# Attention and spectral mixing in one kernel: weights of groups 0 to 2 in four rows a partition, mode products in eight tiles, spectra through a selecting table

## The chip, the cores and the metric

The kernel runs on one core of a Trainium2 chip. The metric is the device time of one execution in microseconds, the median over runs; one more execution was taken with the hardware profiler, and the profile and trace are of that one. Weights, queries, keys and values lie in HBM as float32 and are cast to 16 bits by the transfers.

## The reference

An attention over 8 batches, 8 heads, 576 tokens of width 64, with a bias from a running sum of `s`, feeds a mixing in frequency and a dense layer:

```python
scores = scale * q @ k.T + minimum(-(cum[i] - cum[j]), 0)   # causal; cum = cumsum(maximum(s, 0))
x = softmax(scores) @ v                                     # heads side by side: (8, 576, 512)
X = rfft(x, axis=1)[:, :64]                                 # 64 modes
Y[m] = X[m] @ (w_r[m] + 1j * w_i[m])                        # per mode, 512 x 512, real and imaginary
u = x + irfft(Y, n=576, axis=1)
out = u + maximum(u @ w_ch, 0)
```

`w_r` and `w_i` are 64 x 512 x 512 each, 134 MB together, and are read once.

## The kernel before, in words

**Steps.** The 512 columns are cut into four groups `g` of 128 (two heads each). A main loop runs over 32 steps `n`, eight batches `b` for each group. A step computes the scores of two heads (`scores`, L439 to L459), their product with the values (`av`, L491 to L497, which leaves `x_all`), the transposes of queries and keys for the next step (`transposes`, L400, copied out at L404) and, one step late, the spectrum of what it produced (`fft`, L512 and L522). The order within the step is written out by hand in program order; every engine takes its instructions in that order. Queries and keys come for two steps at a time, into two buffers `qk`.

**Spectrum.** `fft` multiplies the batch's `x_all` (576 tokens by 128 columns) by a table `Ff_sb` of sines, cosines and negative sines, even modes and odd modes in two halves, even columns and odd columns of `x` in two tiles of 64 output rows. Four copies place the result in `xs`: one half of the partitions holds even modes, the other odd modes, and the other half of each column range is zero. So one matrix product over 128 partitions serves two modes, each with two rows of the weights a partition.

**Mode products.** `modes(g, c)` multiplies the spectra of group `g` by the weights of eight modes (chunk `c` of eight): 16 matmuls of 128 rows by 32 columns, streaming 512 columns of weights, on the four column tiles of TensorE (L532). The result, one PSUM bank, is copied or added into `y_acc` (L550, L552). Two banks `aux` are shared by spectra and mode products. The products of group `g` are dealt over the steps of group `g + 1` (`mode_steps`): four chunks in its first step, the others one a step; those of the last group follow the loop, with the inverse transform, the dense layer and the outputs.

**Weights.** A tile `w_sb` holds eight modes of one of `w_r` and `w_i` for one group, 1 MB, in two transfers of 512 KB (`loads_w`): one to partitions 0 to 63, one to 64 to 127, two rows a partition, 64 partitions of four blocks of 2,048 written bytes. The first four tiles go to places that are used later for something else (`x_all`, `y_acc`), the others to three rings of five, three and one tiles. All casting transfers are issued by GpSimd (POOL) at L272, in program order, interleaved by a plan (`on_chip`) with the loads of queries, keys (`qk`) and values (`vr`, `v`). The framework gives POOL's transfers eight completion counters in turn, so an issue waits until the transfer eight before it has landed; it also waits until the buffer that it writes is free. SP issues the constants, one row of running sums a step (L387) and the outputs.

The lines of the profile are those of the listing that follows.

Of the kernel before, what the change touches and what calls it, by code (L numbers as in the profile page):

```python
# [10 lines left out]
FP32 = mybir.dt.float32  # L11
FP16 = mybir.dt.float16
# [7 lines left out]
def kernel(  # L20
# [38 lines left out]
    NK = RV + RV // 2  # L59
    HM = NM // 2  # L60
# [20 lines left out]
    Ff_np = np.zeros((SP, 3 * NM), dtype=np.float16)  # L81
    for h in range(2):
        for i, f in enumerate((np.sin(ang), np.cos(ang), -np.sin(ang))):
            Ff_np[:S, (3 * h + i) * HM : (3 * h + i + 1) * HM] = f[:, h::2]
# [3 lines left out]
    G_np[:, 1, :S] = -(cmv[:, None] * np.sin(ang.T))  # L88
    G_np = np.ascontiguousarray(G_np.reshape(P, SP)[:, :S].astype(np.float16))
# [5 lines left out]
    Ff_np = np.ascontiguousarray(Ff_np.reshape(NT, P, 3 * NM).transpose(1, 0, 2).reshape(P, -1))  # L95
# [15 lines left out]

    xs = [gp.tile([P, 2, 2, 2, 2, B, HM], BF16, name=f"xs{i}") for i in range(2)]
    xs_flat = [t.rearrange("p q k h r b m -> p (q k h r b m)") for t in xs]
    ident16h = gp.tile([P, P], FP16, name="ident16h")
    Ff_sb = gp.tile([P, NT, 3 * NM], FP16, name="Ff_sb")
# [41 lines left out]
    ident16 = ap_.tile([P, P], BF16, name="ident16")  # L157
    negm = ap_.tile([P, NMB + NMA + NL + 59], BF16, name="negm")
# [61 lines left out]
    wq = [(g, c, ri) for g in range(NG) for c in range(NCK) for ri in range(2)]  # L220
# [7 lines left out]
    whole = [xg[:, : 2 * HU], ya[:, HU : 3 * HU], xg[:, 2 * HU : 4 * HU]]  # L228
    whole = [e.rearrange("p (m e) -> p m e", e=DM) for e in whole]
# [12 lines left out]
    def loads_w(upto):  # L242
        todo = []
        while 2 * len(wt) < min(upto, 2 * len(wq)):
            k = len(wt)
            g, c, ri = key = wq[k]
            i = ring_of(k)
            if i is None:
                halves_, t = early[k], whole[k] if k < len(whole) else None
            else:  # L250
                t = (wpool, wpool2, wpool3)[i].tile([P, UM, DM], BF16, name="w_sb", tag="w")
                halves_ = [t[:, x * WM : x * WM + WM] for x in range(2)]
            if k == len(wq) - 1:
                t = None
            src = (moe_w_r, moe_w_i)[ri]
            for m0, m1, d in [(0, MC, t)] if t is not None else [(0, WM, halves_[0]), (WM, MC, halves_[1])]:
                for h in range(2):
                    first = 1 if ri == 1 and c == 0 and m0 + h == 0 else 0
                    todo.append((
                        d[HP * h : HP * h + HP, 2 * first :].rearrange("p (m q) e -> p m (q e)", q=2),  # L260
                        src[
                            c * MC + m0 + h + 2 * first : c * MC + m1 : 2, g * P : (g + 1) * P, :
                        ].rearrange("m (p q) e -> p m (q e)", q=2),
                    ))
            wt[key] = halves_
        return todo
# [88 lines left out]
    nc.vector.tensor_copy(out=ident16, in_=ident16h)  # L355
    for i in range(NQ):
        nc.vector.memset(kt[i][D : D + 1], 1.0)
# [145 lines left out]

    def fft(n):
        if n < 0:
            return
        g, b = divmod(n, B)
        ps = auxpool.tile([P, 2, 3 * HM], FP32, name="ft_ps", tag="aux")
        for T in range(NT):
            nT = tails[T]  # L510
            for q_ in range(2):
                nc.tensor.matmul(  # L512
                    ps[HP * q_ : HP * q_ + HP].rearrange("p h f -> p (h f)"),
                    x_all[:nT, g, b, T, q_::2], Ff_sb[:nT, T, :],
                    start=(T == 0), stop=(T == NT - 1),
                    tile_position=(0, HP * q_), skip_group_check=True,
                )
        for h in range(2):
            for q_ in range(2):
                a = ps[HP * q_ : HP * q_ + HP, h, : 2 * HM].rearrange("p (r m) -> p r m", r=2)  # L520
                a = bass.AP(tensor=a.tensor, offset=a.offset, ap=[a.ap[0], [HM, 2]] + list(a.ap[1:]))
                nc.vector.tensor_copy(out=xs[g % 2][HP * h : HP * h + HP, q_, :, h, :, b, :], in_=a)  # L522

    def modes(g, c, meanwhile=None):


        ps = auxpool.tile([P, DM], FP32, name="yp", tag="aux")
        cols = xs[g % 2].rearrange("p q k h r b m -> p q k (h r b) m")

        def product(ri, q_, cg):  # L530
            k0 = HP if ri == 1 and c == 0 and cg == 0 else 0
            nc.tensor.matmul(  # L532
                ps[32 * cg : 32 * cg + 32, :],
                cols[k0:, q_, 1 - ri, :, c * MC // 2 + cg],
                wt[(g, c, ri)][cg // 2][k0:, 2 * (cg % 2) + q_, :],
                start=(ri == 0 and q_ == 0), stop=(ri == 1 and q_ == 1),
                tile_position=(k0, 32 * cg), skip_group_check=True,
            )

        for x in range(4):  # L540
            ri, y = divmod(x, 2)
            if meanwhile and x in meanwhile:
                meanwhile[x]()
            for z in range(4):
                if meanwhile:
                    product(ri, z // 2, 2 * y + z % 2)
                else:
                    product(ri, y, z)
        if g == 0:
            nc.vector.tensor_copy(out=y_acc[:, c, :], in_=ps)  # L550
        elif g < NG - 1:
            nc.vector.tensor_tensor(out=y_acc[:, c, :], in0=ps, in1=y_acc[:, c, :], op=ALU.add)  # L552
        else:
            yb = spool.tile([P, DM], FP16, name="y_sb", tag="y")
            for cols in halves if c == NCK - 1 else [slice(0, DM)]:
                nc.vector.tensor_tensor(
                    out=yb[:, cols], in0=ps[:, cols], in1=y_acc[:, c, cols], op=ALU.add
                )
            if c >= NCK - 1:
                spread(c, 0, yb)  # L560
            return yb
# [62 lines left out]
    def mode_products(n, half=None):  # L624
        cs = mode_steps.get(n, [])
        for c in cs if half is None else cs[2 * half : 2 * half + 2]:
            modes(c // NCK, c % NCK)

    with tc.tile_pool(name="sc_psum", bufs=2, space=PSUM) as scpool, \
# [8 lines left out]
        for n in range(N):  # L638
            if n in (0, 2):
                nc.vector.memset(xs_flat[n // 2].bitcast(FP32), 0.0)  # L640
# [7 lines left out]
            if n and n % B == 0:  # L648
# [3 lines left out]
                av(n, 0)  # L652
                mode_products(n, 0)
                transposes(n + 1, 0)
                mode_products(n, 1)
                transposes(n + 1, 1)
# [10 lines left out]
            av(n, 0)  # L667
            if i is not None:
# [5 lines left out]
        fft(N - 1)  # L674
    load(loads_w(2 * len(wq)))
# [26 lines left out]
    places += [None, None, old[:, 4 * DM : 8 * DM]]  # L702
# [236 lines left out]
    def first_u():  # L939
# [5 lines left out]
        out=mark[:1], in_=wt[(NG - 1, NCK - 1, 1)][1][HP : HP + 1, WM - 1, :2]  # L945
# [101 lines left out]
```

## Time and profile before

| | |
|---|---|
| runs | 437.28, 437.50, 437.96 us, median 437.5 |
| the profiled execution | 437.52 us, of which the span of its instructions is 435.8 |
| TensorE busy (PE) | 375.4 us, 86% of the span |
| VectorE busy (DVE) | 260.1 us, 60% |
| ScalarE busy (ACT) | 247.1 us, 57% |
| GpSimd busy (POOL) | 141.7 us, 33% |
| transfers of POOL's queue (q0) | 52,560 packets, 81.28 MB written |
| HBM | 163.37 MB read, 9.51 MB written |
| w_r transfers of 512 KB to `w_sb` | 60, 16.5 us from issue to landing in the median |

Rows that give a stretch of time name its start and end, its length, the busy time of PE, PE's weight loads, DVE, ACT and POOL with the number of instructions, the clock granted to TensorE, the share of the 16 DMA engines that packets took, and the GB/s written. Packets overlap on an engine, so that share can pass 1. GB/s count written bytes; casting transfers read twice as many. A row of instructions gives start, length, engine, line, what is written and read, the shapes, how many, and in brackets the idle time before and what ended it. A row of a DMA queue gives packets, MB and their share of 16 engines.

### The profile page before, as it was taken

What the parts mean: (1) busy time and instruction counts of PE and PEld (TensorE: products, weight loads), DVE (VectorE), ACT (ScalarE), POOL (GpSimd) and SP (SyncE); (2) the same over time, 40 slices, a digit from 0 to 9 for tenths busy, and PEclk for the clock granted to TensorE, in tenths of its full rate; (3) what the DMA queues carried; (4) which work ended last, traced back from release to release, by engine and by line L of the source; (5) the groups of instructions that cost most, each with busy time, mean ns of one, the idle gap of its engine ahead of it and who ended that gap; (6) DMA issues with size and microseconds to landing.
All of it is one profiled execution on the core that took longest, in us unless ns stands there. A gap on an engine that the chain in (4) does not pass through costs nothing. (4 is left out here: it accounts for less than half of the span.)

```text
span 435.8 us, 11322 instructions
## 1 busy us (share of the span) xinstructions
PE 375.4 (86%) x4731; PEld 215.4 (49%) x4731; DVE 260.1 (60%) x605; ACT 247.1 (57%) x552; POOL 141.7 (33%) x216
## 2 busy tenths in 40 slices
PE   1699999989999978996496979999998798887994
PEld 1366666556666645654263635555555456442441
DVE  7757767566667665673264446566665654471795
ACT  1387777727767736665163725565565145430895
POOL 6454243141333222322323222322322322210483
PEclk9999999999999998998598878999999999999999
DMA  8999999999999999999999999999999999996698
GB/s 160 208 208 207 208 209 208 212 211 209 209 208 210 207 211 211 210 210 209 208 209 209 210 212 210 209 211 210 212 212 211 212 210 211 212 215 126 209 381 327
DMA packets 59548, 93.14 MB, mean 214 GB/s; under 512 B 8222, under 2 KB 18202, under 8 KB 59498
## 3 DMA queue, kind: packets, MB, share of 16 engines
q0 software_dynamic: 52560, 81.28, 102.9%
q1 hardware_dynamic: 6938, 11.15, 7.3%
q8 instruction: 37, 0.61, 0.5%
q14 instruction: 13, 0.11, 0.1%
HBM read 163.37 MB, written 9.51 MB: 397 GB/s over the span
## 5 line engine op out<-in xcount | busy, mean ns | idle before, releaser
L459 ACT ACTIVATE p_sb<-sc_ps,cumt_sb 128x320 f16<-128x320 f32 (+1 forms) x384 | 161.2, 518 | 31.3 <-PE sc_ps L450 31.3
L450 PE MATMUL sc_ps<-qt,kt 128*64 128x256 bf16 (+3 forms) x640 | 98.4, 301 | 8.8 <-ACT kt L404 8.7
L450 PEld LDWEIGHTS <-kt 128*128 128x128 bf16 (+1 forms) x640 | 50.9, 126 | 72.3 <-issue 38.7
L272 POOL DMA_DIRECT2D w_sb<-in_moe_w_i_dram x62 | 38.3, 619 | 91.3 <-PE yp L532 34.5
L404 DVE COPY qt<-tr_ps 64x576 bf16<-64x576 bf16 x64 | 47.7, 745 | 28.1 <-PE tr_ps L400 28.1
L272 POOL DMA_DIRECT2D w_sb<-in_moe_w_r_dram x60 | 37.0, 619 | 84.4 <-DMA w_sb<-in_moe_w_r_dram 27.2
L496 DVE RECIPROCAL rcp<-av_ps 128x5 f32<-128x5 f32 x64 | 12.5, 195 | 75.5 <-PE av_ps L491 74.5
L439 PE MATMUL sc_ps<-negm,ident 128*128 128x512 bf16 x128 | 52.1, 407 | 0.0
L400 PE MATMUL tr_ps<-ident,qk 64*64 64x64 bf16 x1152 | 32.5, 200 | 18.0 <-DMA qk<-in_k_dram 7.4
L491 PEld LDWEIGHTS <-p_sb 128*128 128x128 f16 x1088 | 42.2, 100 | 8.6 <-issue 3.8
L404 ACT COPY kt<-tr_ps 64x576 bf16<-64x576 bf16 x32 | 22.8, 713 | 37.6 <-DVE qt L404 36.9
L532 PE MATMUL yp<-w_sb,xs 128*32 128x512 bf16 (+1 forms) x480 | 37.9, 406 | 5.3 <-DMA w_sb<-in_moe_w_i_dram 3.6
L421 ACT ACTIVATE p<-sc_ps,cumt 128x64 f16<-128x64 f32 x32 | 10.0, 313 | 54.8 <-PE sc_ps L417 54.8
L400 PEld LDWEIGHTS <-qk 64*64 64x64 bf16 x1152 | 25.0, 114 | 31.7 <-issue 9.0
L522 DVE CAST xs<-ft_ps 64x128 bf16<-64x128 f32 x128 | 36.7, 287 | 6.1 <-PE ft_ps L512 4.7
L442 PE MATMUL sc_ps<-negm,ident 128*128 128x256 bf16 x128 | 36.6, 286 | 0.0
L491 PE MATMUL av_ps<-va,p_sb 128*128 128x65 f16 x768 | 35.9, 196 | 0.0
L497 DVE TENSOR_TENSOR x_all<-av_ps,rcp 128x320 f16<-128x320 f32 x64 | 31.5, 492 | 2.2
L491 PE MATMUL av_ps<-vb,p_sb 128*128 128x65 f16 x320 | 26.6, 198 | 3.8 <-DVE vb L375 3.8
L532 PEld LDWEIGHTS <-xs 128*32 128x32 bf16 (+1 forms) x512 | 17.8, 145 | 19.7 <-DMA w_sb<-in_moe_w_i_dram 6.4
L512 PE MATMUL ft_ps<-Ff_sb,x_all 128*64 128x192 f16 (+1 forms) x320 | 24.0, 263 | 0.8 <-DVE x_all L497 0.8
L404 DVE COPY kt<-tr_ps 64x576 bf16<-64x576 bf16 x32 | 24.4, 763 | 0.4
(120 smaller groups left out, 478.0 us busy)
## 6 DMA issues: line engine op xcount, KB each, us to landing
w_sb<-in_moe_w_r_dram POOLq DMA_DIRECT2D x60, 512.0 KB, 16.5
w_sb<-in_moe_w_i_dram POOLq DMA_DIRECT2D x55, 512.0 KB, 16.4
out_dram<-r_w SPq DMA_DIRECT2D x16, 512.0 KB
qk<-in_q_dram POOLq DMA_DIRECT2D x15, 288.0 KB, 13.3
qk<-in_k_dram POOLq DMA_DIRECT2D x15, 288.0 KB, 15.2
vr<-in_v_dram POOLq DMA_DIRECT2D x14, 256.0 KB, 15.2
x_all<-in_moe_w_r_dram POOLq DMA_DIRECT2D x4, 512.0 KB, 8.6
w_sb<-in_moe_w_i_dram POOLq DMA_DIRECT2D x3, 384.0 KB, 15.1
```

Source lines behind the costliest of these rows:

```text
L272: nc.gpsimd.dma_start(out=dst, in_=src)
L400: nc.tensor.transpose(ps[rows, r, :], src[rows, r, :], ident16[rows, rows])
L404: copy(out=to[:, :, :, half * RH : half * RH + RH], in_=ps[HP * i : HP * i + HP].rearrange("d r (h p) -> d h p r", h=2),)
L439: nc.tensor.matmul(ps[:, : 2 * W], ident16, both, start=True, stop=False, skip_group_check=True)
L442: nc.tensor.matmul(ps[:, S : S + W], ident16, negm[:, NMB + m0 : NMB + m0 + W], start=True, stop=False, skip_group_check=True,)
L450: nc.tensor.matmul(ps[rows, c0 : c0 + i1 - i0], keys, qh[:, i0:i1], start=False, stop=True, skip_group_check=True,)
L459: nc.scalar.activation(out=pt[:, o : o + n_], in_=ps[:, c0 : c0 + n_], func=ACTF.Exp, bias=cumt_sb[:, x, pidx : pidx + 1], scale=0.125,)
L491: nc.tensor.matmul(ps[:, I, :NCH], lhsT, rhs, start=(i == 0), stop=(i == len(todo) - 1), skip_group_check=True,)
L497: nc.vector.tensor_tensor(out=x_all[:, g, b, :, D * h : D * h + D], in0=ps[:, :, :D], in1=rcp.unsqueeze(2).to_broadcast([P, NT, D]), op=AL ...
L512: nc.tensor.matmul(ps[HP * q_ : HP * q_ + HP].rearrange("p h f -> p (h f)"), x_all[:nT, g, b, T, q_::2], Ff_sb[:nT, T, :], start=(T == 0), ...
L522: nc.vector.tensor_copy(out=xs[g % 2][HP * h : HP * h + HP, q_, :, h, :, b, :], in_=a)
L532: nc.tensor.matmul(ps[32 * cg : 32 * cg + 32, :], cols[k0:, q_, 1 - ri, :, c * MC // 2 + cg], wt[(g, c, ri)][cg // 2][k0:, 2 * (cg % 2) + ...
```

## The change

- **Loads.** For groups 0 to 2 a transfer brings four whole modes: each mode takes 32 partitions with four rows a partition, so 128 blocks of 4,096 written bytes go to 128 partitions, and the source is walked mode by mode. Where mode 0 of `w_i` is left out, as before, it is three modes on 96 partitions. The last group keeps two rows a partition, with modes in another choice (every fourth). A tile still holds eight modes and 1 MB, in the same places, rings and plan; the first four tiles are loaded in two transfers each.
- **Spectrum.** `fft` makes one product of 128 rows (sines and cosines of 64 modes) by 128 columns, copied once to `xf_sb`. `fft_pick`, after the next `av`, multiplies it by a table `pick` of zeros, ones and minus ones: 16 matmuls of 32 rows by 96 columns on four column tiles (four matmuls of 64 by 192 for the last group), which put each mode's columns on its partitions with zeros in the other half. One copy takes the result out. The two clearings of `xs` go. The tables are built on DVE behind the identity.
- **Products.** `quads(g, c, ris)` takes 16 modes at a time. For each of `w_r` and `w_i` it makes 32 matmuls of 64 rows by 32 columns on eight tiles of TensorE, into two banks, and each bank is copied or added to `y_acc`. A step that had one chunk now does one of the two `ris`; where two chunks stood in one step, both are done before the banks are taken out. The last group keeps `modes`.
- **Order.** In steps 8, 16 and 24 each of the two transposes moves ahead of the mode products it followed.

```diff
-    wq = [(g, c, ri) for g in range(NG) for c in range(NCK) for ri in range(2)]
+    wq = [(g, c, ri, jj) for g in range(NG - 1) for c in range(NCK // 2) for ri in range(2) for jj in range(2)]
+    wq += [(NG - 1, c, ri, 0) for c in range(NCK) for ri in range(2)]
...
-            for m0, m1, d in [(0, MC, t)] if t is not None else [(0, WM, halves_[0]), (WM, MC, halves_[1])]:
-                for h in range(2):
-                    first = 1 if ri == 1 and c == 0 and m0 + h == 0 else 0
+            rows = slice(g * P, (g + 1) * P)
+            if g < NG - 1:
+                for x in range(2):
+                    m0 = QD * (4 * c + 2 * jj + x)
+                    first = 1 if ri == 1 and m0 == 0 else 0
                     todo.append((
-                        d[HP * h : HP * h + HP, 2 * first :].rearrange("p (m q) e -> p m (q e)", q=2),
-                        src[
-                            c * MC + m0 + h + 2 * first : c * MC + m1 : 2, g * P : (g + 1) * P, :
-                        ].rearrange("m (p q) e -> p m (q e)", q=2),
+                        halves_[x][QP * first :].rearrange("p q e -> p (q e)"),
+                        src[m0 + first : m0 + QD, rows, :].rearrange("m (p q) e -> m p (q e)", q=QD),
                     ))
...
     nc.vector.tensor_copy(out=ident16, in_=ident16h)
+    for t in pick:
+        nq = t.shape[1]
+        nc.vector.memset(t.rearrange("p g k h m -> p (g k h m)").bitcast(FP32), 0.0)
+        for h in range(nq):
+            of_h = ident16.rearrange("p (k m g) -> p g k m", k=2, g=nq)[:, h]
+            nc.vector.tensor_copy(out=t[:, h, :2, h % 2, :], in_=of_h)
+            nc.vector.tensor_scalar(
+                out=t[:, h, 2, h % 2, :], in0=of_h[:, 0], scalar1=-1.0, scalar2=None, op0=ALU.mult
+            )
...
+            nc.tensor.matmul(
+                ps[:, :P], Ff_sb[:nT, T, :], x_all[:nT, g, b, T, :],
+                start=(T == 0), stop=(T == NT - 1), skip_group_check=True,
+            )
+        xf = xf_sb[n % 2]
+        nc.vector.tensor_copy(out=xf, in_=ps[:, :P])
+
+    def fft_pick(n):
...
+        for q_ in range(nq):
+            for h in range(nq):
+                o = P // nq * h
                 nc.tensor.matmul(
...
+                    out[o : o + P // nq, q_, :], xf[:, q_::nq], tab[:, h].rearrange("p k h m -> p (k h m)"),
+                    start=True, stop=True, tile_position=(0, o), skip_group_check=True,
                 )
...
+        nc.vector.tensor_copy(
+            out=spectrum(g)[:, :, :, b, :], in_=ps.rearrange("p (q x m) -> p q x m", q=nq, x=6)
+        )
+
+    def quads(g, c, ris):
+
+        ps = [auxpool.tile([P, DM], FP32, name="yp", tag="aux") for _ in range(2)]
+        cols = spectrum(g).rearrange("p q x b m -> p q (x b) m")
+        for ri in ris:
+            for q_ in range(QD):
+                for j in range(4):
+                    for hp in range(2):
+                        k0 = QP if ri == 1 and c + j + hp == 0 else HP * hp
+                        k1 = HP * hp + HP
+                        c0 = 2 * B * (1 - ri)
+                        nc.tensor.matmul(
+                            ps[hp][32 * j : 32 * j + 32, :],
+                            cols[k0:k1, q_, c0 : c0 + 4 * B, 4 * c + j],
+                            wt[(g, c, ri, j // 2)][j % 2][k0:k1, q_, :],
+                            start=(ri == ris[0] and q_ == 0), stop=(ri == ris[-1] and q_ == QD - 1),
+                            tile_position=(k0, 32 * j), skip_group_check=True,
+                        )
+        for hp in range(2):
+            y = y_acc[:, 2 * c + hp, :]
+            if g == 0 and ris[0] == 0:
+                nc.vector.tensor_copy(out=y, in_=ps[hp])
+            else:
+                nc.vector.tensor_tensor(out=y, in0=ps[hp], in1=y, op=ALU.add)
...
         for n in range(N):
-            if n in (0, 2):
-                nc.vector.memset(xs_flat[n // 2].bitcast(FP32), 0.0)
...
                 fft(n - 1)
                 av(n, 0)
+                fft_pick(n - 1)
+                transposes(n + 1, 0)
                 mode_products(n, 0)
-                transposes(n + 1, 0)
+                transposes(n + 1, 1)
                 mode_products(n, 1)
-                transposes(n + 1, 1)
                 continue
```

## The prediction

> **What bounds it now.** I read the table by stretches first: TensorE (PE) and the DMA share beside each other.
>
> ```profile
> 40.00:50.00 10.00, 9.61 (x131) 5.79 (x130) 6.68 (x19) 7.46 (x18) 4.79 (x8) 1.00 1.16 210
> 210.00:220.00 10.00, 6.79 (x81) 3.68 (x81) 3.38 (x8) 3.53 (x8) 3.36 (x6) 0.53 1.18 207
> 350.00:360.00 10.00, 9.40 (x80) 5.30 (x77) 5.75 (x9) 4.58 (x9) 2.45 (x4) 1.00 1.12 210
> ```
>
> The last two columns never leave 1.11 to 1.26 and 205 to 215 GB/s from 10 to 390 us, while PE falls to 6.79 of 10: the line of transfers is full for 380 us and PE follows it. Its timeline says so too:
>
> ```profile
> 213.21 0.68 PE L400 MATMUL tr_ps<-ident,qk 64*64 64x64 bf16 x17 [3.61 <-DMA qk<-in_k_dram]
> 401.82 0.65 PE L532 MATMUL yp<-w_sb,xs 128*32 128x512 bf16 x4 [0.48 <-DMA w_sb<-in_moe_w_i_dram]
> ```
>
> The second is the last mode product, still waiting for its weights. From there 34 us remain to the end of the span (435.8), outputs mostly, which the change leaves alone. So the time is the line's end plus a fixed tail. The profiled execution took 437.52 us, the median 437.5: the sum below is added to 437.5.
>
> **What a packet costs.** Two stretches of the DMA view, one with small packets, one with weights almost alone:
>
> ```profile
> q0 software_dynamic: 7459, 10.32, 115.9%
> q0 software_dynamic: 3891, 7.50, 111.1%
> ```
>
> The first is 40 to 90 us (800 engine-us on 16 engines), the second 342 to 378 (576). With a ns a packet and b ns a byte: 7,459a + 10.32Mb = 800,000 and 3,891a + 7.50Mb = 576,000, so a = 3.5 ns and b = 0.075. A packet of 2,048 written bytes takes 157 ns of an engine, a transfer of 512 KB (256 of them, 16 an engine) 2.51 us. The change makes 24,384 such packets of groups 0 to 2 into 12,192 of 4,096 bytes, 311 ns each: 12,192 x 3.5 ns / 16 = **-2.7 us**. It is a small difference of large numbers: 0 to -5.
>
> **On how many engines.** Every POOL transfer of before has 64 or 128 as the outermost count of its source, and 4 (3 without mode 0) is new: `m (p q) e -> m p (q e)` puts the modes outside. No row shows POOL's queue with such a source. The nearest is SP's, where `qt<-ncum_dram` reads two rows, from the DMA view of 30 to 300 us:
>
> ```profile
> q1 hardware_dynamic: 108, 0.06, 0.1%
> ...
> qt<-ncum_dram SPq DMA_DIRECT2D x28, 2.2 KB
> ```
>
> 0.06 MB are 27 loads of 2.2 KB, and 108 / 27 = 4 packets each. Were each spread over 16 engines with a completion from each, there would be over 400. Four fit two rows and two completions: dealt by the outermost count, over two engines. So I take four engines for the new transfers; the other end is 16.
>
> [...]
>
> On four engines a transfer takes 32 x 311 ns = 9.9 us instead of 2.5. Four at once carry as much as before, so it costs only where fewer than four are in flight. POOL holds eight at a time (an issue waits for the landing of the one eight before), and at the start most of the eight are small:
>
> ```profile
> 11.79 0.57 POOL L272 DMA_DIRECT2D vr<-in_v_dram  x1 [2.15 <-DMA x_all<-in_moe_w_r_dram]
> 12.36 0.63 POOL L272 DMA_DIRECT2D y_acc<-in_moe_w_i_dram  x1
> ...
> 21.88 0.53 POOL L272 DMA_DIRECT2D vr<-in_v_dram  x1 [1.52 <-DMA y_acc<-in_moe_w_i_dram]
> ```
>
> The 12th issue waits for the 4th transfer, a weight: landed at 11.8, it needs 7.4 us more and shares its engines with less, so near 18.5. The 13th, again a weight, goes out behind it, needs 9.9 us and some 3 to start and land, and the 21st issue waits for that: near 31.5 instead of 21.88. In between only two weight transfers run, on eight engines, beside small ones. Of these 9.6 us between half and all is lost: 5 to 9.6, I take **+8**. Behind it POOL's queue holds mostly weights, four or more in flight: 0 to 3 more, I take 0 (the eight in flight of before are 16.5 us deep against 9.9).
>
> The turn also leaves a remainder: 93 transfers of four blocks and 3 of three are 381 blocks on 16 engines, so 13 get 24 and three 23; the slowest has 0.19 blocks over the mean, 0.19 x 9.9 = **+1.9 us**, and the last group, dealt over all, keeps the difference to the end.
>
> **PE, DVE and order.** All of it is off the path while the line is full; its cover is the wait for data above, and PE's lateness matters where POOL waits for it (10.50 us on `yp` at 342.43, with the line still full).
>
> ```profile
> 104.26 1.09 PE L532 MATMUL yp<-w_sb,xs 128*32 128x512 bf16 x16
> 105.28 0.47 PE L400 MATMUL tr_ps<-ident,qk 64*64 64x64 bf16 x18
> ...
> 108.45 0.72 PE L512 MATMUL ft_ps<-Ff_sb,x_all 128*64 128x192 f16 x10
> ```
>
> And from a step at which a group begins:
>
> ```profile
> 162.35 0.47 PE L400 MATMUL tr_ps<-ident,qk 64*64 64x64 bf16 x18 [1.84 <-DVE kt L404]
> ```
>
> A mode unit is 16 matmuls in 1.02 us (start to next start), four side by side; now 32 of half the rows. Eight side by side make 1.02 again, four 2.04: 0 to +1.0 for each of 24 units. Issue isn't the limit (18 transposes in 0.40 us are 22 ns each, 32 x 22 = 0.7), so I take 0. The spectrum was 0.66 us a step; now five 128x128 (81 ns each by the rows of L718) and 16 small ones at 22 ns, 0.76: +0.1 x 32 = 3 us of PE over the run. DVE: four copies of 287 ns become one of 287 and one of 128x384, between 287 and 683 (L722), some 550: -0.3 x 32 = -10. Units whose halves fall in different steps evict twice: 16 x 0.69 = +11, ahead of the copies of `tr_ps`, perhaps 0.3 us of PE wait in 16 steps (5). Two waits are new on PE, with all its later work queued behind each: a unit takes both banks of `aux`, so in step 8 the second waits for two evictions of the first (1.4 us, of which the transposes cover 0.4); and the picking waits for the copy `xf`, covered by the 1.1 us of `av`. The tables are 14 small operations, some 2 us (two memsets of 192 at the 0.86 ns an element of L640, twelve of 0.1 to 0.2), in DVE's queue ahead of the `kt` memsets and the first copies for the scores, so PE starts 2 us later; two memsets of 1.76 go. In steps 8, 16 and 24 the transposes move ahead of the products, which then cover the waits of 1.84 and 1.16 us: -3 each. PE ends level within 5 us, and the line's own lateness is cover. **0**, bounds -1 to +3; without that cover what PE is late comes on top. SP's row loads wait for the same transposes (L387) and come earlier with them; nothing of theirs is moved.
>
> Sum: -2.7 + 8 + 1.9 + 0 = +7.2: **444.7 us**.
>
> **Rivals.**
> - *All 16 engines carry each transfer.* Then the change does what its shape promises: -2.7, **434.8**, PE's part hidden. For it: all of POOL's rows so far are even. Against: the SP row. 0.2.
> - *The eight tiles run four at a time.* Both row halves of a column write the same 32 partitions of PSUM, in two banks, and no row of before has that with both halves busy. 24 us more of PE, eight of them in steps 24 to 31, where POOL waits for `yp`; the line's lateness covers most, some 2 to 3 come through: **447**. It decides if a unit takes over 1.4 us. 0.12.
> - *Four reads a megabyte apart disturb each other.* Before, an engine's successive reads lie 2 MB apart at the full rate, which speaks against it. If the new ones run at the poorest rate of a stretch, 205 against 212 GB/s, 3% of the 239 us that groups 0 to 2 take (24,384 x 157 ns / 16): +7 on the forecast, **452**. 0.1.
>
> **Numbers.** Forecast 0.58, with 440 to 448 of its own. Measurement of this kernel tells some 0.2% (0.9 us) from no change. Faster: the first rival but for a tenth of it, 0.18. Same: the rest of it and the low end of the forecast, 0.03. Slower: 0.79. The range takes in the first rival with the forecast, since leaving it out with the last two would leave out more than two in ten, and stops at the last one's time: 434.5 to 452.
>
> **What would show it.** DMA packets of group 0 to 2 at 4,096 bytes; transfers `w_sb` landing some 25 us after issue instead of 16.5 and GB/s well under 200 in the stretch from 15 to 35 us say four engines; 2.5 us each and 210 GB/s say 16, and the forecast is wrong. The L532 group's successor at 32 in 1.0 us says eight tiles. The line's end against 402 gives the sum; a DMA share that falls below 1 after 40 us, with POOL waiting for PE, would say that PE has taken over.

## The result and the profile after

| | before | after |
|---|---|---|
| median of the runs | 437.7 us (437.3 to 438.0) | 502.0 us (498.3 to 507.5) |
| ratio | | 1.144 (95%: 1.135 to 1.153) |
| span of the profiled execution | 435.8 us | 497.9 us |
| granted TensorE clock, mean | 0.963 | 0.905 |

The kernel is 64 us slower; the forecast was +7. Here and below, a ratio and its interval leave out runs more than 1.5% above the fastest of their kernel and a median does not, so that a median can lie above what its ratio gives. The table by stretches, same columns as in the prediction (the last two: DMA share, GB/s):

```profile
40.00:50.00 10.00, 10.00 (x158) 6.05 (x156) 5.57 (x14) 7.91 (x20) 2.59 (x4) 0.93 1.03 164
120.00:130.00 10.00, 9.98 (x162) 5.38 (x160) 5.27 (x10) 4.19 (x10) 2.24 (x4) 0.84 1.25 107
210.00:220.00 10.00, 8.15 (x118) 4.77 (x118) 5.02 (x12) 5.16 (x13) 3.44 (x6) 0.83 1.11 199
350.00:360.00 10.00, 8.91 (x150) 5.46 (x147) 7.21 (x16) 6.52 (x15) 2.72 (x4) 1.00 1.08 202
```

The line still bounds the kernel: the share stays above 1, but it now carries 107 to 202 GB/s where it carried 205 to 215. If engines are busy all the time and move half as much, their packets must take longer or carry less; this is the reading that the rest follows. (TensorE's higher busy time at 120 us is no more work: its granted clock there is 0.84, and 0.50 from 110 to 120.) The start is another picture, a share well under that of before (two lines of before, then two of after):

```profile
0.00:20.00 20.00, 7.17 (x77) 4.13 (x77) 14.21 (x50) 4.83 (x9) 11.93 (x24) 1.00 1.04 182
20.00:40.00 20.00, 19.76 (x278) 11.93 (x276) 13.79 (x33) 14.62 (x35) 8.75 (x15) 1.00 1.17 208
```

```profile
0.00:20.00 20.00, 5.82 (x57) 3.31 (x57) 13.92 (x62) 3.52 (x6) 9.13 (x19) 1.00 0.88 154
20.00:40.00 20.00, 12.28 (x131) 6.66 (x131) 6.12 (x15) 7.35 (x17) 7.62 (x13) 0.86 0.82 120
```

There POOL waits as foreseen, for the 12th issue and for the 21st (timeline of POOL):

```profile
17.95 0.58 POOL L289 DMA_DIRECT2D vr<-in_v_dram  x1 [9.82 <-DMA x_all<-in_moe_w_r_dram]
...
33.38 0.55 POOL L289 DMA_DIRECT2D vr<-in_v_dram  x1 [10.01 <-DMA y_acc<-in_moe_w_r_dram]
```

TensorE's timeline, a mode unit with what follows it, and the last mode product:

```profile
173.06 1.10 PE L577 MATMUL yp<-w_sb,xs 64*32 64x512 bf16 x32
174.09 0.47 PE L426 MATMUL tr_ps<-ident,qk 64*64 64x64 bf16 x18
...
462.85 0.65 PE L600 MATMUL yp<-w_sb,xs 128*32 128x512 bf16 x4 [0.45 <-DMA w_sb<-in_moe_w_i_dram]
```

32 products take 1.03 us, as 16 did: eight tiles side by side. The last product starts 61.0 us later than before; behind it lie 35.0 us, before 34.0. So the loss is in the line. What the line moves is told by the queue's row on the page, 52,560 packets and 81.28 MB before:

```profile
q0 software_dynamic: 77296, 81.42, 103.5%
```

12,192 packets should have gone; 24,736 have come. By size, in the trace's packet records, packets of 4 bytes went from 3,152 to 40,080. They can be counted out: before, 197 transfers brought 16 each (3,152), and 195 x 16 are 3,120 now; if each of the 93 four-mode transfers brings 12 x 32 = 384 and each of the three three-mode ones 13 x 32 = 416, the sum is 40,080, all of them. By that count, which names no engine, four engines carry 32 packets each, and each of the other twelve gets as many packets of 4 bytes, called fillers here. They lie 6 to 7 ns apart (start to start, in `mb1` below; 6 is taken here). 36,960 x 6 ns / 16 engines = 13.9 us of the line that the prediction did not have; it is an estimate.

### The profile page after: what moved, and what is told of

It reads as the page before. It is cut to its first block, busy times and chain, and to the rows that moved or that the text cites. A ratio compares the mean times of both kernels' runs of the same rounds, so it can differ in the third digit from the quotient of the medians.

```text
span 497.9 us, 12533 instructions
## 1 busy us (share of the span) xinstructions
PE 405.6 (81%) x5371; PEld 228.5 (46%) x5371; DVE 256.6 (52%) x569; ACT 247.6 (50%) x552; POOL 149.1 (30%) x214
## 5 line engine op out<-in xcount | busy, mean ns | idle before, releaser
L476 PE MATMUL sc_ps<-qt,kt 128*64 128x256 bf16 (+3 forms) x640 | 101.6, 308 | 5.3 <-ACT kt L430 4.8
L426 PE MATMUL tr_ps<-ident,qk 64*64 64x64 bf16 x1152 | 36.5, 208 | 43.0 <-DMA qk<-in_k_dram 22.7
L289 POOL DMA_DIRECT2D w_sb<-in_moe_w_i_dram x62 | 41.4, 669 | 100.2 <-DMA w_sb<-in_moe_w_r_dram 42.0
L289 POOL DMA_DIRECT2D w_sb<-in_moe_w_r_dram x60 | 40.9, 684 | 90.8 <-PE yp L577 23.0
L465 PE MATMUL sc_ps<-negm,ident 128*128 128x512 bf16 x128 | 55.0, 430 | 0.0
L426 PEld LDWEIGHTS <-qk 64*64 64x64 bf16 x1152 | 27.9, 121 | 59.0 <-DMA qk<-in_k_dram 23.9
L517 PEld LDWEIGHTS <-p_sb 128*128 128x128 f16 x1088 | 43.4, 102 | 11.3 <-DVE vb L401 4.4
L577 PE MATMUL yp<-w_sb,xs 64*32 64x512 bf16 (+1 forms) x704 | 32.5, 428 | 6.3 <-DMA w_sb<-in_moe_w_r_dram 2.8
L523 DVE TENSOR_TENSOR x_all<-av_ps,rcp 128x320 f16<-128x320 f32 x64 | 31.5, 491 | 2.2
L289 POOL DMA_DIRECT2D vr<-in_v_dram x22 | 15.5, 707 | 55.0 <-DMA w_sb<-in_moe_w_i_dram 17.9
L589 DVE TENSOR_TENSOR y_acc<-yp,y_acc 128x512 f32<-128x512 f32 x32 | 20.6, 686 | 17.8 <-PE yp L577 17.8
L577 PEld LDWEIGHTS <-xs 64*32 64x32 bf16 (+1 forms) x768 | 16.3, 141 | 20.4 <-issue 16.1
## 6 DMA issues: line engine op xcount, KB each, us to landing
w_sb<-in_moe_w_r_dram POOLq DMA_DIRECT2D x60, 512.0 KB, 18.4
```

The source lines that it names most:

```text
L289: nc.gpsimd.dma_start(out=dst, in_=src)
L426: nc.tensor.transpose(ps[rows, r, :], src[rows, r, :], ident16[rows, rows])
L465: nc.tensor.matmul(ps[:, : 2 * W], ident16, both, start=True, stop=False, skip_group_check=True)
L476: nc.tensor.matmul(ps[rows, c0 : c0 + i1 - i0], keys, qh[:, i0:i1], start=False, stop=True, skip_group_check=True,)
L517: nc.tensor.matmul(ps[:, I, :NCH], lhsT, rhs, start=(i == 0), stop=(i == len(todo) - 1), skip_group_check=True,)
L523: nc.vector.tensor_tensor(out=x_all[:, g, b, :, D * h : D * h + D], in0=ps[:, :, :D], in1=rcp.unsqueeze(2).to_broadcast([P, NT, D]), op=AL ...
```

## The experiments

Times are medians, beside 437.3 to 437.9 us for the kernel before on the same chips. `mb1` to `mb6` contain transfers alone, in stretches with a barrier between; their figures are from the first packet of a stretch, fillers included, to the end of its last data packet, in the trace's packet records. Their table rows give, of the engines, only the busy time of DVE and of POOL. A packet is called undisturbed where it takes what it takes with little else going on: 324 ns for 4,096 written bytes, 173 for 2,048.

**Which part of the change: a_old_loads, b_new_loads, c_16modes, d_skew.** The theories then: "engines" (the four-engine deal), "streams" (reads 1 MB apart), "TensorE".

```diff
 a_old_loads, c_16modes (changed kernel, g < 3): source of a transfer
-  src[m0 : m0 + 4, rows].rearrange("m (p q) e -> m p (q e)", q=4)
+  src[m8 + h : m8 + 8 : 2, rows].rearrange("m (p q) e -> p m (q e)", q=2)              # a
+  src[16 * c : 16 * c + 16, r0 : r0 + 32].rearrange("m (p q) e -> m p (q e)", q=4)     # c
 d_skew: stride between the four modes of a transfer
-  1 MB
+  1 MB + 64 KB
 b_new_loads (kernel before): source of a transfer
+  src[m0 : m0 + 4, rows].rearrange("m (p q) e -> m p (q e)", q=4)
```

> The changed kernel with the weights of groups 0 to 2 fetched by the transfers of before (64 partitions outermost, 2,048 written bytes a packet); everything on TensorE, VectorE and in the order of work stays as changed. Weights land in places that the products don't expect, which changes values only. Theory 'engines' (the four-engine deal of the new transfers is the loss: late start, plus 4-byte filler packets on the twelve other engines) and theory 'streams' (four reads 1 MB apart slow each other down) both put the loss into the transfers: 434 to 440 us, no packets of 4 bytes beyond some 3,100. Theory 'TensorE' (products in eight tiles, picking, order): 490 us or more.

> The kernel before, with the weights of groups 0 to 2 fetched by the new transfers (four modes outermost, 4,096 written bytes a packet); products, spectra and order stay those of before, and get values in places they don't expect. 'Engines' and 'streams': 485 to 505 us, 37,000 more packets of 4 bytes, packets of 4,096 at 350 ns and more on the mean. 'TensorE': 437 to 447 us.

> The changed kernel, each of its transfers taken from sixteen modes (8 partitions of four rows from each) instead of four (32 partitions each): the same packets of 4,096 written bytes, every byte read once, but the outermost count is 16, and sixteen reads 1 MB apart run at once within one transfer. Products get other rows than they should. 'Engines': sixteen engines carry each transfer, no filler packets, start as before: 434 to 441 us. 'Streams': sixteen reads 1 MB apart are no better than four times four: packets of 4,096 stay at 360 ns on the mean or get slower, 465 to 500 us.

> The changed kernel, with the four reads of a transfer 1 MB + 64 KB apart instead of 1 MB (each mode's rows begin 32 rows later than the one before; other rows than the products should get). Everything else, the four engines and the filler packets too, stays. 'Engines': no change from the changed kernel, 495 to 505 us. 'Streams': packets of 4,096 come back to 324 ns and stay there, some 35 us less: 460 to 470 us.

Measured: a 455.3 us (ratio 1.038, 1.032 to 1.043), b 499.3 (1.127, 1.124 to 1.131), c 454.7 (1.036, 1.032 to 1.040), d 502.3 (483.9 to 511.7, no interval). The new transfers alone bring the loss (b); the rest of the change without them does not (a); the same packets on sixteen engines do not (c); moving the reads by 64 KB brings none of it back that these runs could tell, though they spread over 28 us (d; 'streams' had asked for 460 to 470). But a and c came out 15 us above expectation. Both had kept the new form in the few transfers that skip mode 0's imaginary weights (six in a, three in c), and their GB/s fell when those were in flight (a: 148, 192 and 176 GB/s in the stretches of 20 us from 20, 140 and 240 us).

**The same without any four-engine transfer: a2_old_loads, c2_16modes, e_split, f_quadrant.**

```diff
 a2, c2: as a and c, mode 0's imaginary weights fetched like the others
 e_split: four transfers of one mode each, sixteen engines with two packets each
+  halves_[x][32 * i : 32 * i + 32] <- src[m0 + i, rows].rearrange("(p q) e -> p (q e)", q=4)
 f_quadrant: one quadrant of 32 partitions, two modes, partitions outermost
+  t[32 * h : 32 * h + 32] <- src[m0 + h : m0 + h + 5 : 4, rows].rearrange("m (p q) e -> p m (q e)", q=4)
```

> As a_old_loads, but with no four-engine transfer left at all: there, the six transfers of the units that hold mode 0's imaginary weights had kept the new form, and the three dips of GB/s (119 to 176 at 30, 140 and 240 us) came when they were in flight. Mode 0's imaginary weights are fetched too (0.4 MB more, 1.9 us). If a few four-engine transfers cost some 10 us by disturbing all others, this comes to 440 to 446 us, without the dips. If the 17 us of a_old_loads were TensorE's and the order's, it stays at 452 to 457.

> As c_16modes, with no four-engine transfer left: all 96 new transfers have sixteen modes outermost (mode 0's imaginary weights fetched too). Packets of 4,096 bytes on sixteen engines, against 2,048 bytes in a2_old_loads: by the price of a packet 2.7 us less than a2_old_loads, if packet time counts; the same if the loss is elsewhere. 437 to 444 us.

> The changed kernel, each new transfer of four modes sent as four transfers of one mode (32 partitions, 128 KB): the same rows in the same places, 4,096-byte packets, outermost count 32, so sixteen engines with two packets each and no filler. 288 more issues of POOL at some 0.67 us, and eight in flight are 1 MB instead of 4 MB. If the four-engine deal is the loss: 440 to 450 us with the line near 195 to 210 GB/s; if eight small transfers in flight are too few, 460 to 490 and DMA share under 1.

> The changed kernel with correct values, its weights in the same places, but each transfer fills one quadrant of 32 partitions with two modes (partitions outermost): 256 KB, 4,096-byte packets, sixteen engines, no filler. Eight in flight are 2 MB instead of 4 MB, and POOL issues 96 more. 438 to 444 us if eight such transfers still keep the line full (as in c2_16modes, which gave 440.6 with 512 KB); 450 and more if the line runs dry where POOL waits for TensorE.

Measured: a2 444.1 us (1.015, 1.011 to 1.020), c2 440.6 (1.007, 1.004 to 1.011), e 465.4 (1.065, 1.062 to 1.067), f 439.6 (1.005, 1.003 to 1.008). Six four-engine transfers had cost `a` 11 us, more than 13 with the weights that a2 fetches besides. c2 is 3.5 us below a2, near the 2.7 that the halved packet count was to give; their runs overlap a little (440.0 to 443.6 and 442.2 to 446.8). f does what the change was to do, four rows a partition at sixteen engines, with every weight where the products expect it: 62 us faster than the changed kernel and still 2 us slower than the one before (437.0 to 442.7 against 437.0 to 438.6). e is the lesser remedy: its transfers of 128 KB land 5.5 us after issue, so eight in flight are a thin line.

**The start: h_start.** a2 with the first eight weight transfers in the new form.

> a2_old_loads with its first eight weight transfers (four units, those that lie ahead of the first steps) in the four-engine form, the rest as before: the term of the prediction for the start, +8 (5 to 9.6), alone. 444 + 8 = 452 us (449 to 454) if that term was right; 455 to 460 if the disturbance of other transfers adds to it.

Measured 459.4 us (1.049, 1.046 to 1.051), 15.3 over a2. Table by stretches, a2 and then h:

```profile
20.00:40.00 20.00, 19.07 (x301) 11.89 (x301) 11.81 (x29) 15.56 (x38) 8.55 (x15) 1.00 1.17 207
40.00:60.00 20.00, 19.76 (x328) 12.47 (x325) 11.94 (x31) 15.52 (x36) 8.16 (x14) 1.00 1.19 208
```

```profile
20.00:40.00 20.00, 12.37 (x131) 6.71 (x131) 6.13 (x15) 7.35 (x17) 7.45 (x13) 0.87 0.80 117
40.00:60.00 20.00, 19.12 (x316) 11.90 (x315) 11.38 (x29) 15.13 (x36) 5.48 (x9) 0.96 1.19 175
```

Two losses show: engines without work (share 0.80 up to 40 us) and, with the share back at 1.19, 175 GB/s instead of 208, the slow packets again. Counted by how many of sixteen data packets were missing in flight, up to 60 us, the idle part is 8.6 us more than before; the prediction's +8 was that part.

**What slows the packets: mb1, mb2, mb3.**

> Transfers alone, no other work; the output is zeros. Three four-engine transfers one at a time, then stretches of sixteen transfers of 512 KB, a barrier between: (1) form of before; (2) four modes by 32 partitions; (3) sixteen modes by 8; (4) four modes, reads skewed by 64 KB within and by 16 KB between transfers; (5) forms of before and four modes in turn; (6) eight modes by 16; (7) two modes by 64; (8) four modes, the first four of growing height (8, 16, 24, 32 partitions), so that transfers in flight are at different partitions; (9) sixteen modes, every fourth one four modes. Single transfer: four packets of 4,096 at a time, 10 us, 384 fillers in chains of 32. Theory 'lockstep' (engines that write the same partition at the same time slow each other): (2), (4) and (7) slow, (7) most, (8) at 324 ns. Theory 'fillers': (7) worst (896 a transfer), then (2), (4), (8) alike, then (6) (128), and (1) and (3) at the full rate. Theory 'reads': (4) faster than (2).

In order, three single transfers aside: 40.7 us (form of before), 53.3 (four modes by 32), 40.7 (sixteen by 8), 56.5 (four, skewed), 75.1 (before and four in turn, 8 MB all the same), 43.0 (eight by 16), 55.9 (two by 64), 50.2 for nine tenths of the bytes (four, staggered), 44.4 (every fourth one four). A single four-engine transfer, then the stretches of the old and of the new form:

```profile
51.00:60.00 9.00, 0.00 (x0) 0.00 (x0) 1.00 0.26 52
80.00:110.00 30.00, 0.00 (x0) 4.89 (x8) 1.00 1.12 211
125.00:170.00 45.00, 0.00 (x0) 5.37 (x8) 1.00 1.14 174
```

The first line is four engines of sixteen: a quarter of the share, a quarter of the rate. The last is the fault in pure form, share as before, rate 18% lower, with no other work in the kernel. Skewed reads are no faster, and in turn with the old form it is worst.

> Transfers alone, 8 MB in each of seven stretches: (1) four modes by 32 partitions, 4,096 bytes a packet: 384 fillers per 512 KB, 56 us as in mb1; (2) four modes by 16 partitions, 8,192 bytes: still four engines, 192 fillers; (3) four modes by 32, 2,048 bytes: four engines, 768 fillers per 512 KB; (4) eight modes by 16, 2,048 bytes: eight engines, 256 fillers; (5) eight modes by 8, 8,192 bytes: eight engines, 64 fillers; (6) two modes in 32 partitions, partitions outermost, 256 KB; (7) one mode in 32 partitions, 128 KB. If the fillers' number sets the loss (13 us for 384): (2) 49, (3) 69 and more, (4) 51, (5) 45. If the number of engines sets it: (2) and (3) as (1), (4) and (5) 46. (6) 43; (7) 43 to 50, by POOL's issues.

Measured 94.1, 79.3, 50.1, 44.5, 58.7, 47.2 and 42.2 us. The third stretch has twice the fillers and undisturbed packets (median 173 ns, mean 179): fillers cost their own time (190 GB/s in the middle of that stretch, 220 to 250 us, against 211 without them) but slow nobody. The first, the very form that took 53 us in mb1, took 94: mostly 720 to 880 ns a packet (means of 4 us). It had been undisturbed (322 ns) while the output was written beside it, up to 51 us, and was slow from then on to its end.

> Transfers alone, 6 MB in each stretch, sixteen streams of 8 partitions (sixteen engines, no filler) whose reads lie 64, 128, 256, 512, 1,024, 2,048, 1,032, 1,040, 1,056, 1,088, 1,152 and 1,280 KB apart; then four streams of 32 partitions 1,024 KB apart, once with successive transfers 4 MB apart and once with four successive transfers 256 KB apart within the same four modes. If the addresses that are read at the same time set the rate: 256 KB (the pitch at which mb2's first stretch, at 760 to 860 ns a packet, had its four transfers in flight) near half the rate, 60 us, others 32 us; the last two stretches 40 and 70 us. If addresses don't matter and only the four-engine form does: all sixteen-stream stretches 32 us, the last two alike.

Measured 30.5 to 31.6 us at all twelve pitches; 40.2 and 43.4 for four streams. Which addresses are read together does not matter at these pitches.

**Where engines meet: mb4, m_halves, mb5, mb6.**

> Transfers alone, 8 MB in each stretch, all four streams 1 MB apart on four engines, so fillers and reads are of one kind. (1) 4 x 32 partitions, the first third beside the writing of the output as in mb2's first stretch, but with successive transfers 4 MB apart; (2) 4 x 8 partitions of 8,192 bytes, four successive transfers to the four different quadrants; (3) the same, all to one quadrant; (4) 4 x 16 partitions of 4,096 bytes, to the two halves in turn; (5) the same, all to one half; (6) 4 x 32 again, nothing beside it; (7) and (8) 4 x 8 of 4,096 bytes, four quadrants in turn, and one. If engines that write the same partitions at the same time slow each other: (3) at half the rate of (2) or worse, (5) slower than (4), (8) slower than (7), (1) near 94 us because the output's writing brought the engines into step. If only the four-engine form and its fillers matter: (2) and (3), (4) and (5), (7) and (8) alike, (1) and (6) 53 us apart from the overlap.

Measured 110.4, 45.5, 49.3, 46.9, 52.5, 53.0, 56.5 and 59.3 us. Each pair goes the way of "same partitions", (2) before (3), (4) before (5), (7) before (8), but by 5 to 12%, not by half. That the traffic at the start brought the engines of (1) into step, so that they work at the same place of their transfers at the same time, is my reading; no row shows where an engine stands. (1) and (6) are one form, once with the writing of the output beside its first part and once without:

```profile
56.00:72.00 16.00, 0.00 (x0) 0.00 (x0) 1.00 1.22 77
346.00:394.00 48.00, 0.00 (x0) 7.58 (x12) 1.00 1.12 169
```

> The changed kernel, each of its transfers of 128 partitions sent as two of 64 (four modes by 16 partitions, other rows than the products should get; mode 0's imaginary weights too, 0.4 MB): still four engines a transfer, as many fillers per byte (384 for 512 KB), the same packets; but the transfers in flight lie on two halves in turn, so that fewer engines write the same partitions. The start gains too: a transfer takes 5 us instead of 10. If engines in step on the same partitions are the largest share (some 30 us): 460 to 480 us, and the time that packets take above the undisturbed 324, 192, 173 and 60 ns, summed over 40 to 400 us and divided by 16, falls from 54 to below 30 us. If the form and its fillers are what slows the packets: 485 to 498 by the start alone, and the sum stays over 45.

Measured 491.5 us (1.117, 1.110 to 1.124); the time above undisturbed, summed and divided by 16, fell from 54 to 46 us only. The part of the 4,096-byte packets in that sum hardly fell, from 26 to 25. That is against "same partitions" as I had put it.

> Transfers alone: sixteen pieces on sixteen engines, 32 transfers a stretch after a first stretch that only gets past the output's writing; pieces of 4,096, then 2,048, then 1,024 written bytes, each size once to sixteen partitions and once all to a single partition, so that sixteen engines write one partition at the same time and there are no fillers. If a partition takes writes at a rate of its own (some 260 ns for 4,096 bytes, from mb4's first stretch: 1,050 ns a packet with four engines in step), the single-partition stretch takes 32 x 16 x 0.26 = 134 us at 4,096, packets near 4 us, half and a quarter of it at 2,048 and 1,024; the sixteen-partition ones stay at POOL's issues, some 17 to 20 us. If engines don't hinder each other at a partition, both alike.

Measured, single partition: 67.2, 30.8 and 17.0 us; sixteen partitions: 16.5, 15.5 and 15.4, POOL's issues. With one partition a transfer, successive transfers to successive partitions, 2.1 MB take 67.2 us:

```profile
95.00:155.00 60.00, 0.00 (x0) 11.62 (x24) 1.00 1.24 30
```

31 GB/s, 131 ns for 4,096 bytes, where an engine alone offers 13.4 (4,096 bytes in 305 ns; the four of mb1's single transfer moved 52 together). By that, two engines fit and four must wait: 4 x 131 = 524 ns, an estimate. But mb4's first stretch stood near 1,050, as if eight met; four engines share a partition there at most.

> Transfers alone, 128 KB each, 32 a stretch (4.2 MB), pieces of 4,096 written bytes, the first stretch only to get past the output's writing. A single partition took 31 GB/s in mb5. [...] Theory 'partition' (31 GB/s each partition, no sharing between partitions): four engines are on different partitions in every transfer and up to four transfers meet, so that 1, 4, 8, 16 and 32 apart are all alike, 34 us.

Measured: sixteen partitions 1 apart 55.5 us, 4 apart 22.5; four engines at 4, 8, 16, 32 and 1 apart: 79.2, 79.1, 77.1, 77.4 and 119.1. Two things went otherwise than meant: pieces that lie side by side went as one packet (8 KB and 32 KB), and at 4, 8 and 1 apart one transfer ran at a time, so that four engines were at work there and sixteen at 16 and 32 apart. So the times don't compare, and the packets only within each of the two groups. The stretch 16 apart, and 4 apart:

```profile
322.00:380.00 58.00, 0.00 (x0) 12.89 (x23) 1.00 1.07 55
146.00:206.00 60.00, 0.00 (x0) 14.13 (x29) 1.00 0.25 53
```

| four engines a transfer, partitions | engines at work | packet of 32 KB, median |
|---|---|---|
| 4 or 8 apart | 4 | 2.43 us (undisturbed) |
| 1 apart | 4 | 3.59 us, from 2.43 to 4.86 |
| 16 or 32 apart | 16 | 9.48 and 9.49 us |

At 1 apart each partition of a transfer has one engine, and yet they hinder each other (3.59 us against 2.43): the unit is more than a partition. Sixteen neighbours do too (887 ns against 624 for 8 KB at 4 apart). At 16 and at 32 apart the sixteen engines together get 55 GB/s, less than twice the 31 of mb5: by that ratio nearly two units, 27 GB/s each if it is two, an estimate. At 4 and 8 apart four engines were undisturbed at 53 GB/s together, which bounds nothing from above. Which partitions make up a unit these runs do not show, nor is its rate settled: 31 GB/s in mb5, 27 by the estimate from 16 and 32 apart.

With a unit of more than one partition more than four can meet. By 131 ns an engine a packet takes 524 ns where four meet, 786 for six and 1,050 for eight, and mb2's and mb4's first stretches show mostly 720 to 880 and 990 to 1,070. These are estimates, and how many met is open: by 27 GB/s the same counts give 600, 900 and 1,200 ns, and the 77 GB/s of mb4's first stretch are 2.5 to 2.8 units at 31 to 27, about six engines a unit.

In the changed kernel the median was 535 ns from 110 to 120 us and 632 from 120 to 130, the worst of its stretches of 10 us; over the run it is the undisturbed 324, and a tenth of the packets took more than 438. The trace shows one thing more: of the 54 us above undisturbed, only 26 lie in the 4,096-byte packets; 14 lie in the 512-byte packets of the values and 12 in those of queries and keys, transfers that the change left alone and that before took no longer than undisturbed. The four-engine transfers slow what runs beside them.

Transfers that go to two halves in turn should have met less often, and that m_halves took away so little these runs do not explain. That the kernel's own slow stretches are such meetings is inferred from the runs of transfers alone; the kernel's trace does not tell where a packet writes.

**TensorE's part: g_quadrant_fft, k_late_pick.** In a2's last steps the picking waits, although `av` lies between:

```profile
319.86 0.36 PE L562 MATMUL ft_ps<-pick,xf 128*64 128x192 bf16 x4 [0.39 <-DVE xf L548]
```

```diff
 g (on f_quadrant): fft ahead of the second transposes; at a group's start the picking behind the first
 k (on f_quadrant), late steps:
                 first_product(i, 0)
+                fft_pick(n - 1)
                 first_transposed(i, 1)
```

> f_quadrant with the spectrum's first product put ahead of the second transposes, and the picking behind the transposes in the steps that begin a group, so that 0.4 us more of TensorE's work lie between the copy xf and the picking that waits for it (0.39 us of wait in each late step). If that wait is what makes TensorE's steps 12.1 us instead of 11.6, 2 to 5 us less than f_quadrant; if it is covered elsewhere, the same.

> f_quadrant with the picking put behind the first products of the late steps (z of 128x512), which then cover the wait for xf: 0.39 us in each of the five late steps that show it. If TensorE's pace sets those steps, 2 us less than f_quadrant: 437 to 438.5, level with before. If not, 439.5 as f_quadrant. It beats before only if the packets' 2.7 us come through beside it: 435 to 436.

Measured: g 445.3 us (1.018, 1.015 to 1.020), k 439.6 (1.006, 1.003 to 1.010), f 439.6. In g one wait of the picking is left, but the scores wait for `kt` 14 times instead of 4; what makes it 5.7 us slower is not shown. In k the picking's wait is covered and comes back further on, for a copy of ScalarE:

```profile
303.05 0.38 PE L666 MATMUL xt_ps<-ident16h,x_all 128*128 128x128 f16 x4 [0.38 <-ACT z L660]
```

So k's late steps still take 12.2 us, and it could not tell what the wait is worth. No version beats the kernel before.

## Why the prediction was right or wrong

**What bounds (right).** The line does, before and in the changed kernel; its end moved by 61 us and the tail by 1.

**Packets, -2.7 (borne out).** c2 against a2: -3.5, with runs that overlap a little.

**Four engines (right).** The single transfer in mb1 takes 11.1 us on a quarter of the engines (forecast 9.9; share 0.26, 52 GB/s), and the rival with sixteen engines fell.

**Start, +8 (mechanism right, under-sized).** 17.95 and 33.38 us against the forecast 18.5 and 31.5. The idle engines cost 8.6, as reckoned, the whole 15.3, because the transfers that did run were slowed as well.

**"Four at once carry as much as before, so it costs only where fewer than four are in flight": 0 later, 0 to 3. This is the step that failed.** From h_start to the changed kernel are 42.6 us, and the 88 transfers behind the start are all that differs in the line. So the term that was put at 0 was some 43. Fillers are 12.7 of them (88 x 384 x 6 ns / 16, an estimate). The rest, 30, goes to slow packets, or about 34 if the halved packets (-3.2) and mode 0's weights that h still fetches (1.3) are put back. Before, hardly a packet waited for another: the time above undisturbed came to 0.9 us in 40 to 400 us, and after to 54 (more than the loss, since packets overlap on an engine). The sum had a price for the packet and the number of engines, but took the engines for independent of each other and the twelve idle ones for free. That the four-engine form brings both losses is shown: a2, c2 and f, without such a transfer, have neither fillers nor many slow packets (1.9 to 3.4 us above undisturbed). Why the packets are slow, that engines meet where they write, is inferred.

**Remainder, +1.9.** Not to be told apart in these runs. That the engines are taken in turn, on which the term rests, was the author's assumption: the packet records name no engine.

**TensorE, DVE and order, 0 (-1 to +3).** a2 is 6.4 us slower, 1.9 of it for mode 0's weights (0.4 MB at 209 GB/s): +4.5, outside the bound. The eight tiles were right (1.03 us). The products of the spectrum were right too, 0.49 + 0.30 us against 0.76. Wrong was "covered by the 1.1 us of `av`": five late steps show 0.36 to 0.40 us of wait, and steps 28 to 30 take 12.1 us instead of 11.6. k_late_pick only moved the wait, so that what it costs the median stays open. The three times -3 at steps 8, 16 and 24 did not come: in a2 steps 8, 16 and 24 take 15.1, 12.1 and 17.3 us, 12.8 each before. Wrong, too, was that the full line covers what TensorE is late. The prediction had named the place, POOL's wait for `yp`; there the line runs dry in a2 (before, then a2, whose profiled run took 446.8 us):

```profile
350.00:355.00 5.00, 4.41 (x45) 2.55 (x42) 2.79 (x5) 1.76 (x4) 1.84 (x3) 1.00 1.11 209
350.00:355.00 5.00, 5.00 (x36) 1.43 (x29) 1.61 (x4) 0.00 (x0) 1.62 (x3) 0.50 0.63 107
353.38 1.24 POOL L293 DMA_DIRECT2D w_sb<-in_moe_w_r_dram  x2 [11.64 <-PE yp L604]
```

With the shallower dips from 300 to 320 us and from 355 to 360, where such waits of some 10 us end too, a2's line misses 1.1 MB against 209 GB/s, some 5 us. In f it dips at 290 and at 345 us (145 GB/s), some 2 us, and with the packets' gain its line ends at 401.0 us, where that of before ended at 401.4. But the last mode product, which waited for its weights before and in the changed kernel (0.48 and 0.45 us), waits no longer:

```profile
403.17 0.65 PE L608 MATMUL yp<-w_sb,xs 128*32 128x512 bf16 x4
```

It starts 1.35 us later than before. So in f TensorE, not the line, sets the end. Which operation makes it late stays open, and so does what the granted clock of 0.50 adds in the line of a2 above.

**Rivals.** Eight tiles four at a time: fell. Reads a megabyte apart: the right sign, some packets slow, but the wrong end of the transfer. mb3 shows that the reads' addresses don't matter, d_skew agrees within its spread, and the rival's 7 us were a fifth of what the slow packets cost.

**What would show it.** GB/s well under 200 at the start came (120). A landing time of 25 us did not: 18.4 in place of 16.5. A share below 1 behind 40 us with POOL waiting for TensorE did not come in the changed kernel before its end, where the slow line covered TensorE, but it came in a2.

## What to carry to other kernels

Read the outermost count of a transfer's source (four modes there ran at a quarter of the engines' share, 0.26, in mb1; with sixteen, in c2, no fillers came), not only the size of its packets, and keep partitions outermost: f_quadrant has the large packets at sixteen engines by turning two dimensions round. A transfer on few engines was not paid for by having more of them in flight; ask what the engines that run at once write, and whether they come at the same time to the same few partitions (31 GB/s in mb5) or to some 16 or 32 apart (55 in mb6). Take off a cover, here the slow line, and look again at what it covered. And when a share stays at 1 while the bytes fall, look at how long one packet takes before looking for a missing transfer.

## What the hardware showed unasked

A POOL transfer of four modes brought, beside its 128 packets of data, 384 of four bytes by the count above, 32 for each of twelve engines. Sixteen engines that write one partition a transfer get 31 GB/s together (mb5), where each alone offers 13.4, and sixteen engines on partitions 16 or 32 apart get 55 (mb6). The same four-engine form over as many bytes took 53 us or 110, and the changed kernel's runs spread over 9 us where those of before stay within 0.7; that this is a matter of phase, of which engines happen to meet, is inferred.
